# Three of four sequence transforms computed as cosine and sine halves in a spectral MLP kernel

## The chip, the cores and the metric

The kernel runs on one core of a Trainium2 chip. Five engines work side by side: TensorE (PE, matrix products; PEld is its weight load, which overlaps), VectorE (DVE), ScalarE (ACT), GpSimd (POOL) and SyncE (SP, which issues DMAs). The metric is the device time of one execution in microseconds (us), the median of several runs. Lower is better.

## The reference

```python
# x: (4, 3008, 256); w_in: (256, 2048); w_out: (2048, 256)
X = np.fft.fft(x, axis=1)
X = np.fft.fft(X, axis=2)
attn = X.real.astype(np.float32)          # two-dimensional transform, real part
h = attn.reshape(-1, 256) @ w_in
g = h * (1.0 / (1.0 + np.exp(-h)))
out = (g @ w_out).astype(np.float32)
```

## The kernel before

The transform over the 256 features is folded into `w_in` once, at the start; the transform over the 3008 rows is done on the chip as matrix products. Because the result is real and symmetric, only 1506 sequence frequencies of each of the four batches are made. They fall into four classes (`CLASS`, line 40): class 0 with 376 columns, class 1 with 378, classes 2 and 3 with 376 each. Sixteen transforms (batch b, class k, number c = 4b + k) feed a two-layer network that runs over columns in chunks: one chunk per class in batch 0, then three chunks of 502 columns for each other batch.

**Precision.** Products are made in fp32r with operands split into a high and a low part, so each logical product is three matmuls: high by high, high by low, low by high. `xh`, `xl` are the parts of a transform's operand; `uvh`, `uvl` those of its result, on which the network works.

**A step.** The main loop (from line 735) runs over the steps (chunk, f), f from 0 to 15, each for 128 hidden units. On PE a step issues `first` (six matmuls, lines 409 to 411) and `second` of the step three earlier (`LAG`; twelve matmuls, lines 463 to 470). DVE does three sums from PSUM in `act` (lines 420 to 422), ACT the SiLU and a rounding (433, 434), DVE the low part in `rest` (446).

**A turn.** At 15 fixed steps (`turns`, lines 683 to 691) a transform is issued on PE after `second` (`transform`, line 327), between two steps. The first of all transforms (batch 0, class 0) is made apart, at the start. The result goes to one of the two PSUM buffers `pq`, which `first` uses too, in turn. Then `spread` (line 367) empties it: ACT writes `uvh` (380), ACT copies row 0 to a small tile `row` (383), from which a DMA of SP's queue broadcasts it to 128 partitions as `ub` (384), and DVE writes `uvl` (387). The buffer is needed again by `first` two steps later. `ub` and the parts of `uv` are needed where their chunk begins, four steps after the turn at the least.

**A transform's matmuls.** Classes 0, 2 and 3 multiply three blocks of operand rows (`x3`, made by `operand`, line 250) by three table blocks of 376 columns, for two halves i of the features, each as three matmuls: 18 matmuls of 376 columns. Class 1 makes its even and odd outputs apart: 30 matmuls of 190 or 188 columns. Every matmul has its own weight load of 128 columns; the operand is the weight, and the table moves. `operand` runs in pieces between steps on DVE, ACT rounds to `xh` (315), and POOL makes `xl` (322).

**Order.** Everything is issued in an order written out by hand: each engine works its own queue strictly in that order, and side work is handed out by budgets per step (`drain`, line 490).

Of the kernel before, what the change touches and what calls it, by code (L numbers as in the profile page):

```python
# [24 lines left out]
F32 = mybir.dt.float32  # L25
F32R = mybir.dt.float32r
# [5 lines left out]
AF = mybir.ActivationFunctionType  # L32
ALU = mybir.AluOpType
# [3 lines left out]
Q4, H = S // 4, S // 8  # L37
NC = 1506
NT = B * NC
CLASS = ((0, 376), (376, 378), (754, 376), (1130, 376))  # L40
# [10 lines left out]
def fft_mlp(ctx, tc, x1, x2, x2_first, w_in, w_out, te, to, t2, t2f, rot1, rot2, dft, out):  # L51
    nc = tc.nc
    ctx.enter_context(tc.manual_schedule())
    tt = nc.vector.tensor_tensor
# [34 lines left out]
    t2f_sb = wts.tile([128, 2, 3, 376], F32, tag="t2", name="t2f")[:, 0]  # L89
    rot_sb = [wts.tile([128, 2, 2], F32, name=f"rot_sb{i}") for i in range(2)]  # L90

    wo_raw, wo_wide = {}, {}
# [58 lines left out]
    ends = slice(0, 129, 128)  # L151


    def fold_sums(k, i, ps=every):
        tt = nc.gpsimd.tensor_tensor
        sm = fold_tile("sm", k, i)[ps]
        gs = [raw_x.pop((k, i, h))[ps] for h in range(2)]

        def finish(h):
            nc.scalar.activation(sm[:, h, :, ends], gs[h][:, 0:2, ends], AF.Copy)  # L160

        for h, g in enumerate(gs):
            tt(g[:, 0:2], g[:, 0:2], g[:, 2:4], op=ALU.add)
            tt(sm[:, h, :, 1:128], g[:, 0:2, 1:128], g[:, 0:2, 129:], op=ALU.add)
            tt(sm[:, h, :, 129:], g[:, 0:2, 1:128], g[:, 0:2, 129:], op=ALU.subtract)
            yield 9
        finish(0)
        yield 9
        finish(1)
        ready.add(("sm", k, i, ps.stop))  # L170
# [79 lines left out]
    def operand(c):  # L250
# [8 lines left out]
        x3 = xf[:, :768].rearrange("p (a d) -> p a d", a=3)  # L259
        if k == 0:  # L260
            sm, sm2 = folded["sm", 0, b], folded["sm", 1, b // 2]
            tt(x3[:, 0:2, 0:129], sm[:, :, 0, 0:129], sm[:, :, 1, 0:129], op=ALU.subtract)
            for h in range(2):
                tt(x3[:, 1 - h, 129:], sm[:, h, 0, 129:], sm[:, h, 1, 129:], op=ALU.subtract)
            yield 0.7
            for h in range(2):
                rows = (lo, up)[h]
                tt(x3[rows, 2, 0:129], sm2[hs, h, 0, 0:129], sm2[hs, h, 1, 0:129], op=ALU.subtract)
                tt(x3[rows, 2, 129:], sm2[hs, 1 - h, 0, 129:], sm2[hs, 1 - h, 1, 129:], op=ALU.subtract)
            yield 0.8  # L270
        elif k == 1:
            sm, sm2 = folded["sm", 0, b], fold_tile("sm", 1, b // 2)
            piece = 0.3
            tt(sm[:, :, 0], sm[:, :, 0], sm[:, :, 1], op=ALU.add)
            yield piece
            if b:
# [18 lines left out]
            yield piece  # L295
            for par, op in ((0, ALU.add), (1, ALU.subtract)):
                tt(l0[:, par, 0:129], sm[:, 0, 0:129], sm[:, 1, 0:129], op=op)
                tt(l0[:, 1 - par, 257:], sm[:, 0, 129:], sm[:, 1, 129:], op=op)
                yield piece
                tt(c0[lo, par, 0:129], sm2[hs, 0, 0, 0:129], sm2[hs, 1, 0, 0:129], op=op)  # L300
                tt(c0[up, 1 - par, 129:], sm2[hs, 0, 0, 129:], sm2[hs, 1, 0, 129:], op=op)
                yield piece
        else:
            ri, ri2 = folded["ri", 0, b], folded["ri", 1, b // 2]
# [22 lines left out]
    def transform(c, po):  # L327

        b, k = divmod(c, 4)
        x = operands.pop(c)  # L330
        n = CLASS[k][1]
        def sl(a):
            return slice(a, a + 128)

        def product(dst, terms, part):

            w = dst.shape[-1]
            for j, (rows, a, t, blk) in enumerate(terms):
                for p in range(2 - part):
                    nc.tensor.matmul(dst, x[part][rows, sl(a)], t[rows, p, blk, :w], start=j + p + part == 0,  # L340
                                     stop=part == 1 and j == len(terms) - 1)

        if k == 1:
            for i in range(2):
                for par, t, at, m in ((0, tabs["te"], 0, 190), (1, tabs["to"], 190, 188)):
                    l, z = 384 * par, 768 + 256 * par
                    if i == 0:
                        terms = [(every, l, t, 0), (every, z, t, 2)]
                    else:
                        terms = [(every, l + 128, t, 0), (every, l + 256, t, 1), (every, z + 128, t, 2)]  # L350
                    for part in range(2):
                        product(po[:, i, at:at + m], terms, part)
        else:
            t = tabs[{0: "t2", 2: "te", 3: "to"}[k]]
            for part in range(2):
                for i in range(2):
                    product(po[:, i, :n], [(every, 256 * a + 128 * i, t, a) for a in range(3)], part)

    chunks = {}

# [6 lines left out]
    def spread(c, po):  # L367

        b, k = divmod(c, 4)
        o, n = CLASS[k]  # L370
        o += b * NC
        parts = []
        for j, (at, m) in enumerate(zip(STARTS, CHUNKS)):
            lo, hi = max(o, at), min(o + n, at + m)
            if lo < hi:
                uvh, uvl, ub, _, _ = chunk(j)
                src, dst = slice(lo - o, hi - o), slice(lo - at, hi - at)
                parts.append((uvh[:, :, dst], uvl[:, :, dst], ub[:, dst], src))
        for uvh, _, _, src in parts:
            nc.scalar.activation(uvh, po[:, :, src], AF.Copy)  # L380
        for _, _, ub, src in parts:
            row = fold_p.tile([1, 512], F32, tag="half", name="row", bufs=3)[:, :src.stop - src.start]
            nc.scalar.activation(row, po[0:1, 1, src], AF.Copy)  # L383
            nc.sync.dma_start(
                out=ub, in_=row.unsqueeze(0).to_broadcast([1, 128, src.stop - src.start]))
        for uvh, uvl, _, src in parts:
            tt(uvl, po[:, :, src], uvh.bitcast(F32), op=ALU.subtract)  # L387


    def spread_first(po):  # L390
        uvh, uvl, ub, n, _ = chunk(0)
# [331 lines left out]
    for q, n in enumerate((0, 1, 2, 3, 4, 5, 7, 9)):  # L723
# [6 lines left out]
        if q >= FULL // 2:  # L730
            fills.setdefault(n - 1, []).append((clear_wo, q))
            after.setdefault(n + 1, []).append((high_wo, q))
            fills.setdefault(n + 2, []).append((low_wo, q))

    for n in range(len(steps) + LAG):
        c, f = steps[min(n, len(steps) - 1)]
        if n < len(steps):
# [46 lines left out]
    return base % S, (-base) % S  # L784


_S1 = np.arange(128)
_S2 = np.concatenate([np.arange(128, 189), [188] * 3])


def _tables():
    w1 = np.where(_S1 == 0, 0.5, 1.0)[:, None]
    w2 = np.where(_S2 == 188, 0.5, 1.0)[:, None]
    w2[61:] = 0

    def cs(m):
        def f(s, fn):
            return fn(2 * np.pi * (np.outer(s, m) % 752) / 752)

        t = np.zeros((128, 3, len(m)))  # L800
        t[:, 0], t[:, 1] = w1 * f(_S1, np.cos), -w1 * f(_S1, np.sin)
        t[:64, 2], t[64:, 2] = w2 * f(_S2, np.cos), -w2 * f(_S2, np.sin)
        return t

    m = np.arange(376)

    def g(s):
        return np.cos(2 * np.pi * (np.outer(s, 2 * m + 1) % 1504) / 1504)

    t2 = np.zeros((128, 3, 376))  # L810
    t2[:, 0], t2[:, 1] = w1 * g(_S1), w1 * g(H - _S1)
    t2[:64, 2], t2[64:, 2] = w2 * g(_S2), w2 * g(H - _S2)

    def rot(s):
        b = 2 * np.pi * np.stack([s, H - s], 1) / S
# [12 lines left out]
    got = {  # L828
        "te": parts(cs(np.arange(0, 752, 2))), "to": parts(cs(np.arange(1, 752, 2))), "t2": parts(t2), "t2f": t2,
        "rot1": rot(_S1), "rot2": np.concatenate([rot(_S2)] * 2), "dft": dft,  # L830
    }
    return {k: np.ascontiguousarray(v, dtype=np.float32) for k, v in got.items()}
# [15 lines left out]

def _columns():

    m = np.arange(376)
    k = np.concatenate([4 * m + 2, 8 * np.arange(190), 8 * np.arange(188) + 4, 8 * m + 1, 8 * m + 5])
    neg = np.concatenate([m % 2 == 1, np.ones(378, bool), np.zeros(752, bool)])
    keep = np.arange(NC) != 376 + 189
    k1 = np.where(neg, -k, k) % S
    return keep, (-k1) % S, k1
# [28 lines left out]
```

## Time and profile before

| | us |
|---|---|
| median of 3 runs | 878.06 |
| lowest and highest | 877.62, 878.19 |
| profiled execution, whole time | 877.21 |
| its span, first to last instruction | 875.4 |
| PE busy in it | 866.1 (99%) |
| DVE busy | 706.2 (81%) |
| ACT busy | 508.9 (58%) |
| POOL busy | 197.9 (23%) |

A busy PE is not a PE at its peak, since matmuls are pipelined and their recorded durations overlap. What a matmul costs the engine is read from the spacing of the starts, or from the chain of waits, where each piece stands with the time that it adds.

### The profile page before, as it was taken

The numbers are of one execution on the slowest core, as the hardware profiler recorded it, in microseconds if no ns is written. First come the engines' busy times: TensorE is split into PE (matmuls) and PEld (weight loads), VectorE is DVE, ScalarE is ACT, GpSimd is POOL, SyncE is SP. The second block draws the span as 40 slices with busy tenths as digits, with TensorE's granted clock in tenths as the row PEclk, the third lists the DMA queues.
The fourth block names the chain that finished last, engine by engine and source line by source line (L and its number), as shares of the span: only waits on it lengthen the run. The fifth ranks groups of instructions, "written<-read, shape, count | busy, mean of one in ns | idle before, by whom it ended". The sixth has DMA issues, their size and how long they took to land.

```text
span 875.4 us, 11058 instructions
## 1 busy us (share of the span) xinstructions
PE 866.1 (99%) x4138; PEld 750.2 (86%) x4138; DVE 706.2 (81%) x994; ACT 508.9 (58%) x646; POOL 197.9 (23%) x243
## 2 busy tenths in 40 slices
PE   7999999999999999999999999999999999999998
PEld 6789999999998888888888888888888888888886
DVE  5999888888897887879778877888877877777774
ACT  4677756565765564557566455557546555455554
POOL 3475541312522220243312310050300110000000
PEclk9999999999999999999999999999999999999999
DMA  9955342236231433224225201323011021200101
GB/s 333 313 177 84 106 53 53 37 58 93 10 106 26 76 77 58 44 11 112 34 30 124 9 1 50 56 48 57 1 8 49 0 10 48 10 0 5 44 1 47
DMA packets 23413, 53.81 MB, mean 61 GB/s; under 512 B 3648, under 2 KB 12224, under 8 KB 22976
## 3 DMA queue, kind: packets, MB, share of 16 engines
q1 hardware_dynamic: 19632, 38.62, 20.4%
q0 software_dynamic: 3728, 14.49, 8.6%
q8 instruction: 32, 0.52, 0.3%
q14 instruction: 21, 0.17, 0.1%
HBM read 37.86 MB, written 12.34 MB: 57 GB/s over the span
## 4 chain that ended last, share of the span: by engine, by line
PE 97%; DMA 1%; DVE 1%; SPq 1%; issue 0%; ACT 0%; DVEq 0%
PE acc L470 20%; PE acc L464 20%; PE acc L463 20%; PE pq L409 10%; PE pq L410 10%; PE pq L411 10%; PE pq L340 5%; PE acc L461 2%; DMA minus<-in_x_dram 1%; PE pw L533 1%; PE pq L597 0%; SPq L74 0%; SPq L569 0%; DVE sm L204 0%; DVE sm L200 0%
## 5 line engine op out<-in xcount | busy, mean ns | idle before, releaser
L433 ACT ACTIVATE h<-h 128x1004 f32<-128x1004 f32 (+3 forms) x204 | 199.3, 977 | 303.6 <-DVE h L422 300.4
L463 PE MATMUL acc<-gh,woh 128*128 128x502 f32 (+2 forms) x808 | 302.2, 374 | 0.0
L464 PE MATMUL acc<-gh,wol 128*128 128x502 f32 (+2 forms) x808 | 302.2, 374 | 0.0
L446 DVE TENSOR_TENSOR gl<-h,gh 128x1004 fp32r<-128x1004 f32 (+3 forms) x204 | 237.9, 1167 | 14.7 <-ACT gh L434 14.0
L420 DVE SCALAR_TENSOR_TENSOR h<-ub,a,pq 128x502 f32<-128x502 f32 (+2 forms) x208 | 144.8, 696 | 96.7 <-PE pq L411 92.5
L470 PE MATMUL acc<-gl,woh 128*128 128x502 f32 (+2 forms) x808 | 210.3, 374 | 0.0
L434 ACT ACTIVATE gh<-h 128x1004 fp32r<-128x1004 f32 (+3 forms) x204 | 199.4, 977 | 6.5
L464 PEld LDWEIGHTS acc<-gh,wol 128*128 128x128 f32 x808 | 152.4, 189 | 22.4
L463 PEld LDWEIGHTS acc<-gh,woh 128*128 128x128 f32 x808 | 152.0, 188 | 22.3
L470 PEld LDWEIGHTS acc<-gl,woh 128*128 128x128 f32 x808 | 149.6, 188 | 23.2
L409 PE MATMUL pq<-uv,abh 128*128 128x502 f32 (+2 forms) x416 | 157.7, 379 | 0.0
L410 PE MATMUL pq<-uv,abh 128*128 128x502 f32 (+2 forms) x416 | 154.8, 372 | 0.0
L411 PE MATMUL pq<-uv,abl 128*128 128x502 f32 (+2 forms) x416 | 154.6, 372 | 0.0
L421 DVE TENSOR_TENSOR h<-h,pq 128x502 f32<-128x502 f32 (+2 forms) x208 | 132.7, 638 | 7.2
L422 DVE TENSOR_TENSOR h<-h,pq 128x502 f32<-128x502 f32 (+2 forms) x208 | 132.6, 638 | 7.2
L322 POOL TENSOR_TENSOR xl<-xf,xh 128x256 fp32r<-128x256 f32 x53 | 53.0, 1027 | 365.4 <-ACT xh L315 306.1
L409 PEld LDWEIGHTS pq<-uv,abh 128*128 128x128 f32 x416 | 78.1, 188 | 12.3 <-DVE h L422 0.5
L410 PEld LDWEIGHTS pq<-uv,abh 128*128 128x128 f32 x416 | 78.2, 188 | 11.7
L411 PEld LDWEIGHTS pq<-uv,abl 128*128 128x128 f32 x416 | 78.1, 188 | 11.4
L234 POOL TENSOR_TENSOR ri<-ri,raw 128x256 f32<-128x256 f32 x24 | 23.1, 978 | 57.6 <-ACT ri L229 57.3
L478 ACT ACTIVATE o<-acc 128x502 f32<-128x502 f32 (+2 forms) x52 | 27.9, 559 | 9.8 <-PE acc L470 7.7
L387 DVE TENSOR_TENSOR uv<-pq,uv 128x752 fp32r<-128x752 f32 (+4 forms) x21 | 14.5, 716 | 21.2 <-ACT row L383 21.1
(113 smaller groups left out, 472.5 us busy)
## 6 DMA issues: line engine op xcount, KB each, us to landing
raw<-in_x_dram SPq DMA_DIRECT2D x22, 512.0 KB, 6.3
raw<-in_x_dram POOLq DMA_DIRECT2D x20, 512.0 KB, 7.5
out_dram<-o SPq DMA_DIRECT2D x36, 251.0 KB, 2.2
win<-in_w_in_dram SPq DMA_DIRECT2D x8, 512.0 KB, 8.1
wo<-in_w_out_dram SPq DMA_DIRECT2D x8, 512.0 KB, 8.0
out_dram<-o SPq DMA_DIRECT2D x12, 188.0 KB, 2.3
ub<-row SPq DMA_DIRECT2D x8, 188.0 KB, 8.6
te<-in_te_dram POOLq DMA_DIRECT2D x1, 1128.0 KB, 5.5
```

The source lines that it names most:

```text
L409: nc.tensor.matmul(po, abh[:, i, fs], uvh[:, i, :n], start=True, stop=False)
L410: nc.tensor.matmul(po, abh[:, i, fs], uvl[:, i, :n], start=False, stop=False)
L411: nc.tensor.matmul(po, abl[:, i, fs], uvh[:, i, :n], start=False, stop=True)
L420: stt(p[:, :n], ub[:, :n], a128[f // 2][:, f % 2:f % 2 + 1], pq[:, 0, :n], op0=ALU.mult, op1=ALU.add)
L421: tt(h[:, 0, :n], p[:, :n], pq[:, 1, :n], op=ALU.add)
L422: tt(h[:, 1, :n], p[:, :n], pq[:, 1, :n], op=ALU.subtract)
L433: nc.scalar.activation(h[:, sg, :n], h[:, sg, :n], AF.Silu)
L434: nc.scalar.activation(gh[:, sg, :n], h[:, sg, :n], AF.Copy)
L446: tt(gl[:, sg, :n], g[:, sg, :n], gh[:, sg, :n].bitcast(F32), op=ALU.subtract)
L463: nc.tensor.matmul(po, wo[0][f // 2][:, f % 2, es], gh[:, sg, :n], start=f == 0, stop=False)
L464: nc.tensor.matmul(po, wo[1][f // 2][:, f % 2, es], gh[:, sg, :n], start=False, stop=False)
L470: nc.tensor.matmul(accs[c][i][:, :n], wo[0][f // 2][:, f % 2, es], gl[:, sg, :n], start=False, stop=f == NF - 1)
```

## The change

For classes 0, 2 and 3 the tables keep only half of the output columns (`w`, 188, or 190 for class 2). The transform writes two parts side by side into the same PSUM tile: for classes 2 and 3 a cosine part and a sine part, for class 0 the part of the even and of the odd rows. The first operand block is multiplied by the table of the first part, `w` columns wide, the second block by that of the second part, and the third block, which holds the remaining rows of both, by a table of `2 * w` columns. `spread` then copies the second part to SBUF (ACT, tile `q`), makes sum and difference on DVE into a new SBUF tile `wide`, and takes `uvh` and the broadcast row from `wide`; the low part `uvl` is made one step later, after the next `act`. Output columns come in another order, so the host tables and the gather of the output are permuted to match. Class 1 keeps its products; only its table layout differs.

```diff
-_S1 = np.arange(128)
+_S1 = np.concatenate([np.arange(0, 128, 2), np.arange(1, 128, 2)])
...
 # fold_sums
-            tt(sm[:, h, :, 129:], g[:, 0:2, 1:128], g[:, 0:2, 129:], op=ALU.subtract)
+            tt(sm[:, 1 - h, :, 129:], g[:, 0:2, 1:128], g[:, 0:2, 129:], op=ALU.subtract)
 # operand, class 0
-            tt(x3[:, 0:2, 0:129], sm[:, :, 0, 0:129], sm[:, :, 1, 0:129], op=ALU.subtract)
-            for h in range(2):
-                tt(x3[:, 1 - h, 129:], sm[:, h, 0, 129:], sm[:, h, 1, 129:], op=ALU.subtract)
-            yield 0.7
-            for h in range(2):
-                rows = (lo, up)[h]
-                tt(x3[rows, 2, 0:129], sm2[hs, h, 0, 0:129], sm2[hs, h, 1, 0:129], op=ALU.subtract)
-                tt(x3[rows, 2, 129:], sm2[hs, 1 - h, 0, 129:], sm2[hs, 1 - h, 1, 129:], op=ALU.subtract)
+            for par, src in enumerate((lo, up)):
+                for h, dst in enumerate((lo, up)):
+                    tt(x3[dst, par], sm[src, h, 0], sm[src, h, 1], op=ALU.subtract)
+                yield 0.8
+            for h, dst in enumerate((lo, up)):
+                tt(x3[dst, 2], sm2[hs, h, 0], sm2[hs, h, 1], op=ALU.subtract)
             yield 0.8
 # transform
-        def product(dst, terms, part):
+        def product(dst, a, t, at, part, start=False, stop=False):
             w = dst.shape[-1]
+            for p in range(2 - part):
+                nc.tensor.matmul(dst, x[part][:, a:a + 128], t[:, p, at:at + w], start=start and p + part == 0,
+                                 stop=stop and part == 1)
...
-            t = tabs[{0: "t2", 2: "te", 3: "to"}[k]]
+            t, w = {0: (tabs["t2"], 188), 2: (tabs["te"], 190), 3: (tabs["to"], 188)}[k]
             for part in range(2):
                 for i in range(2):
-                    product(po[:, i, :n], [(every, 256 * a + 128 * i, t, a) for a in range(3)], part)
+                    both = po[:, i, :2 * w], 512 + 128 * i, t, 2 * w, part
+                    if part == 0:
+                        product(*both, start=True)
+                    product(po[:, i, :w], 128 * i, t, 0, part)
+                    product(po[:, i, w:2 * w], 256 + 128 * i, t, w, part)
+                    if part:
+                        product(*both, stop=True)
 # spread
+        if k == 1:
+            wide = po
+        else:
+            wide = xs.tile([128, 2, 376], F32, tag="wide", name="wide")
+            w, m, skip = (190, 189, 1) if k == 2 else (188, 188, 0)
+            q = fold_p.tile([128, 2, 190], F32, tag="half", name="q", bufs=3)
+            nc.scalar.activation(q[:, :, :w], po[:, :, w:2 * w], AF.Copy)
+            tt(wide[:, :, :m], po[:, :, :m], q[:, :, :m], op=ALU.add)
+            tt(wide[:, :, m:], po[:, :, skip:skip + n - m], q[:, :, skip:skip + n - m], op=ALU.subtract)
         for uvh, _, _, src in parts:
-            nc.scalar.activation(uvh, po[:, :, src], AF.Copy)
+            nc.scalar.activation(uvh, wide[:, :, src], AF.Copy)
         for _, _, ub, src in parts:
-            row = fold_p.tile([1, 512], F32, tag="half", name="row", bufs=3)[:, :src.stop - src.start]
-            nc.scalar.activation(row, po[0:1, 1, src], AF.Copy)
+            row = wide[0:1, 1:2, src]
+            if k == 1:
+                row = fold_p.tile([1, 1, 512], F32, tag="half", name="row", bufs=3)[:, :, :src.stop - src.start]
+                nc.scalar.activation(row, po[0:1, 1:2, src], AF.Copy)
...
-        for uvh, uvl, _, src in parts:
-            tt(uvl, po[:, :, src], uvh.bitcast(F32), op=ALU.subtract)
+        def lower_parts():
+            for uvh, uvl, _, src in parts:
+                tt(uvl, wide[:, :, src], uvh.bitcast(F32), op=ALU.subtract)
+        if k == 1:
+            lower_parts()
+        return k != 1 and lower_parts
 # main loop
             act(c, f, fills.get(n, ()))
+            if lowers:
+                lowers = lowers()
...
-            spread(turn, new)
+            lowers = spread(turn, new)
 # tables: 3 blocks of 376 columns become 5 blocks of w (te, to) or 4 of 188 (t2)
-            tabs[name] = pool.tile([128, 2, 3, 376], F32R, name=name)
+            tabs[name] = pool.tile([128, 2, t.shape[-1]], F32R, name=name)
-        tabs["t2"] = wts.tile([128, 2, 3, 376], F32R, tag="t2", name="t2")
+        tabs["t2"] = wts.tile([128, 2, 752], F32R, tag="t2", name="t2")
```

## Rows read from the trace of the kernel before

**Rows 1.** Page: busy us of each engine, share of span, instructions.
```profile
PE 866.1 (99%) x4138; PEld 750.2 (86%) x4138; DVE 706.2 (81%) x994; ACT 508.9 (58%) x646; POOL 197.9 (23%) x243
```

**Rows 2.** Waits of PE, all of them: us in total, times, longest.
```profile
PE pq L597 <- DVE xf L207: 2.0, 2, 1.1
PE pq L587 <- POOL wof L573: 1.8, 1, 1.8
PE pw L533 <- DVE wf L82: 1.5, 1, 1.5
```

**Rows 3.** Page: chain that ended last, shares of the span by line.
```profile
PE acc L470 20%; PE acc L464 20%; PE acc L463 20%; PE pq L409 10%; PE pq L410 10%; PE pq L411 10%; PE pq L340 5%; PE acc L461 2%; DMA minus<-in_x_dram 1%; PE pw L533 1%; PE pq L597 0%; SPq L74 0%; SPq L569 0%; DVE sm L204 0%; DVE sm L200 0%
```

**Rows 4.** The same chain in order of time: start us, us, what.
```profile
121.83 0.69 PE acc L470 x4
122.53 3.08 PE pq L340 x18
...
435.81 3.33 PE pq L340 x30
...
487.39 0.92 PE acc L470 x4
...
749.70 3.09 PE pq L340 x18
```

**Rows 5.** Line 340, weight loads: ns min/median/max, first and last start, forms.
```profile
L340 PEld LDWEIGHTS pq<-te,xh x88: 187/188/192, 65.6 to 699.0; 128*128 128x128 f32 x88
```

**Rows 6.** Span and mean granted TensorE clock of the core.
```profile
core 0: 875.4 us, clock 1.000
```

**Rows 7.** Timeline after a class 2 turn: start us, us, instruction [idle before].
```profile
489.96 1.21 DVE L446 TENSOR_TENSOR gl<-h,gh 128x1004 fp32r<-128x1004 f32 x1 [0.76 <-ACT gh L434]
...
491.24 0.40 PE L409 MATMUL pq<-uv,abh 128*128 128x502 f32 x1
...
491.44 0.86 ACT L380 ACTIVATE uv<-pq 128x500 fp32r<-128x500 f32 x2 [1.51 <-PE pq L340]
...
492.73 1.00 DVE L387 TENSOR_TENSOR uv<-pq,uv 128x500 fp32r<-128x500 f32 x2 [1.56 <-ACT row L383]
...
494.32 0.73 DVE L420 SCALAR_TENSOR_TENSOR h<-ub,a,pq 128x502 f32<-128x502 f32 x1
...
495.34 0.39 PE L409 MATMUL pq<-uv,abh 128*128 128x502 f32 x1
```

**Rows 8.** Timelines of four engines after the class 2 turn of batch 0.
```profile
125.45 0.33 PE L409 MATMUL pq<-uv,abh 128*128 128x378 f32 x1
128.57 0.34 PE L409 MATMUL pq<-uv,abh 128*128 128x378 f32 x1
...
125.65 0.80 ACT L380 ACTIVATE uv<-pq 128x752 fp32r<-128x752 f32 x1 [1.64 <-PE pq L340]
...
126.83 0.48 SPq L384 DMA_DIRECT2D ub<-row  x1
...
136.06 0.61 DVE L420 SCALAR_TENSOR_TENSOR h<-ub,a,pq 128x376 f32<-128x376 f32 x1 [0.49 <-PE pq L411]
```

**Rows 9.** DMA issues: count, KB each, median us from issue to landing.
```profile
ub<-row SPq DMA_DIRECT2D x8, 188.0 KB, 8.6
```

**Rows 10.** By tile: ns min/median/max of instructions like the added ones.
```profile
L394 ACT ACTIVATE uv<-pq x2: 451/468/484, 25.1 to 25.9; 128x376 fp32r<-128x376 f32 x2
L396 DVE TENSOR_TENSOR uv<-pq,uv x2: 540/545/550, 25.6 to 26.7; 128x376 fp32r<-128x376 f32 x2
...
L309 DVE TENSOR_TENSOR xf<-ri x8: 408/415/422, 110.7 to 705.7; 64x256 f32<-64x256 f32 x8
```

**Rows 11.** Timelines of POOL and PE before the class 0 turn of batch 1.
```profile
193.97 2.85 POOL L322 TENSOR_TENSOR xl<-xf,xh 128x256 fp32r<-128x256 f32 x3 [29.60 <-ACT xh L315]
...
202.07 1.19 PE L340 MATMUL pq<-t,xl 128*128 128x376 f32 x6
```

**Rows 12.** Waits of DVE, the longest: us in total, times, longest.
```profile
DVE h L420 <- PE pq L411: 92.5, 130, 1.3
```

More of the change, by code (lines that the diff above doesn't have):

```diff
@@ L88, in fft_mlp @@
     tabs = {}
-    t2f_sb = wts.tile([128, 2, 3, 376], F32, tag="t2", name="t2f")[:, 0]
+    t2f_sb = wts.tile([128, 1504], F32, tag="t2", name="t2f")[:, :1128].rearrange("p (a k) -> p a k", a=3)
     rot_sb = [wts.tile([128, 2, 2], F32, name=f"rot_sb{i}") for i in range(2)]
@@ L272, in operand @@
             sm, sm2 = folded["sm", 0, b], fold_tile("sm", 1, b // 2)
-            piece = 0.3
+            piece, h0 = 0.3, 1 if b else 0
             tt(sm[:, :, 0], sm[:, :, 0], sm[:, :, 1], op=ALU.add)
@@ L297, in operand @@
                 tt(l0[:, par, 0:129], sm[:, 0, 0:129], sm[:, 1, 0:129], op=op)
-                tt(l0[:, 1 - par, 257:], sm[:, 0, 129:], sm[:, 1, 129:], op=op)
+                tt(l0[:, 1 - par, 257:], sm[:, h0, 129:], sm[:, 1 - h0, 129:], op=op)
                 yield piece
                 tt(c0[lo, par, 0:129], sm2[hs, 0, 0, 0:129], sm2[hs, 1, 0, 0:129], op=op)
-                tt(c0[up, 1 - par, 129:], sm2[hs, 0, 0, 129:], sm2[hs, 1, 0, 129:], op=op)
+                tt(c0[up, 1 - par, 129:], sm2[hs, h0, 0, 129:], sm2[hs, 1 - h0, 0, 129:], op=op)
                 yield piece
@@ L330, in transform @@
         x = operands.pop(c)
-        n = CLASS[k][1]
-        def sl(a):
-            return slice(a, a + 128)
-        def product(dst, terms, part):
+        def product(dst, a, t, at, part, start=False, stop=False):
             w = dst.shape[-1]
[L338 to L341, printed above, removed]
+            for p in range(2 - part):
+                nc.tensor.matmul(dst, x[part][:, a:a + 128], t[:, p, at:at + w], start=start and p + part == 0,
+                                 stop=stop and part == 1)
@@ L343, in transform @@
         if k == 1:
             for i in range(2):
[L345 to L350, printed above, removed]
+                for par, t, dst in ((0, tabs["te"], po[:, i, :190]), (1, tabs["to"], po[:, i, 190:378])):
+                    w = dst.shape[-1]
+                    l, z = 384 * par + 128 * i, 768 + 256 * par + 128 * i
@@ L351, in transform @@
                     for part in range(2):
-                        product(po[:, i, at:at + m], terms, part)
+                        product(dst, l, t, 0, part, start=True)
+                        if i:
+                            product(dst, l + 128, t, w, part)
+                        product(dst, z, t, 4 * w, part, stop=True)
         else:
-            t = tabs[{0: "t2", 2: "te", 3: "to"}[k]]
+            t, w = {0: (tabs["t2"], 188), 2: (tabs["te"], 190), 3: (tabs["to"], 188)}[k]
             for part in range(2):
@@ L378, in spread @@
                 parts.append((uvh[:, :, dst], uvl[:, :, dst], ub[:, dst], src))
+        if k == 1:
[7 more added lines that the diff above has]
+            tt(wide[:, :, m:], po[:, :, skip:skip + n - m], q[:, :, skip:skip + n - m], op=ALU.subtract)
         for uvh, _, _, src in parts:
-            nc.scalar.activation(uvh, po[:, :, src], AF.Copy)
+            nc.scalar.activation(uvh, wide[:, :, src], AF.Copy)
         for _, _, ub, src in parts:
-            row = fold_p.tile([1, 512], F32, tag="half", name="row", bufs=3)[:, :src.stop - src.start]
-            nc.scalar.activation(row, po[0:1, 1, src], AF.Copy)
-            nc.sync.dma_start(
-                out=ub, in_=row.unsqueeze(0).to_broadcast([1, 128, src.stop - src.start]))
-        for uvh, uvl, _, src in parts:
-            tt(uvl, po[:, :, src], uvh.bitcast(F32), op=ALU.subtract)
+            row = wide[0:1, 1:2, src]
+            if k == 1:
+                row = fold_p.tile([1, 1, 512], F32, tag="half", name="row", bufs=3)[:, :, :src.stop - src.start]
+                nc.scalar.activation(row, po[0:1, 1:2, src], AF.Copy)
+            nc.sync.dma_start(out=ub, in_=row.to_broadcast([1, 128, src.stop - src.start]))
+        def lower_parts():
[4 more added lines that the diff above has]
+        return k != 1 and lower_parts
     def spread_first(po):
@@ L733, in fft_mlp @@
             fills.setdefault(n + 2, []).append((low_wo, q))
+    lowers = None
     for n in range(len(steps) + LAG):
@@ L784, in _rows @@
     return base % S, (-base) % S
-_S1 = np.arange(128)
-_S2 = np.concatenate([np.arange(128, 189), [188] * 3])
+_S1 = np.concatenate([np.arange(0, 128, 2), np.arange(1, 128, 2)])
+_S2 = np.concatenate([np.arange(128, 189, 2), [188], np.arange(129, 188, 2), [188] * 2])
+_PAD = [31, 62, 63]
+_M0 = np.concatenate([np.arange(188), 375 - np.arange(188)])
+_M2 = np.concatenate([np.arange(189), 376 - np.arange(1, 188)])
 def _tables():
@@ L793, in _tables @@
     w2 = np.where(_S2 == 188, 0.5, 1.0)[:, None]
-    w2[61:] = 0
+    w2[_PAD] = 0
     def cs(m):
@@ L798, in f @@
             return fn(2 * np.pi * (np.outer(s, m) % 752) / 752)
-        t = np.zeros((128, 3, len(m)))
-        t[:, 0], t[:, 1] = w1 * f(_S1, np.cos), -w1 * f(_S1, np.sin)
-        t[:64, 2], t[64:, 2] = w2 * f(_S2, np.cos), -w2 * f(_S2, np.sin)
+        w = len(m)
+        t = np.zeros((128, 5 * w))
+        t[:, :w], t[:, w:2 * w] = w1 * f(_S1, np.cos), -w1 * f(_S1, np.sin)
+        t[:64, 2 * w:3 * w], t[64:, 3 * w:4 * w] = w2 * f(_S2, np.cos), -w2 * f(_S2, np.sin)
+        t[:, 4 * w:] = t[:, 2 * w:3 * w] + t[:, 3 * w:4 * w]
         return t
-    m = np.arange(376)
     def g(s):
[L808 to L812, printed above, removed]
+        return np.cos(2 * np.pi * (np.outer(s, 2 * _M0 + 1) % 1504) / 1504)
+    t2f = np.zeros((128, 3, 376))
+    t2f[:, 0], t2f[:, 1] = w1 * g(_S1), w1 * g(H - _S1)
+    t2f[:64, 2], t2f[64:, 2] = w2 * g(_S2), w2 * g(H - _S2)
+    t2 = np.zeros((128, 752))
+    for k in range(2):
+        own, tail = slice(64 * k, 64 * k + 64), slice(32 * k, 32 * k + 32)
+        for h in range(2):
+            dst = slice(64 * h, 64 * h + 64)
+            t2[dst, 188 * k:188 * k + 188] = t2f[own, h, :188]
+            t2[64 * h + 32 * k:64 * h + 32 * k + 32, 376 + 188 * k:564 + 188 * k] = t2f[dst, 2, :188][tail]
     def rot(s):
@@ L828, in _tables @@
     got = {
-        "te": parts(cs(np.arange(0, 752, 2))), "to": parts(cs(np.arange(1, 752, 2))), "t2": parts(t2), "t2f": t2,
+        "te": parts(cs(2 * np.arange(190))), "to": parts(cs(2 * np.arange(188) + 1)), "t2": parts(t2), "t2f": t2f,
         "rot1": rot(_S1), "rot2": np.concatenate([rot(_S2)] * 2), "dft": dft,
@@ L849, in _columns @@
 def _columns():
-    m = np.arange(376)
-    k = np.concatenate([4 * m + 2, 8 * np.arange(190), 8 * np.arange(188) + 4, 8 * m + 1, 8 * m + 5])
-    neg = np.concatenate([m % 2 == 1, np.ones(378, bool), np.zeros(752, bool)])
+    k = np.concatenate([4 * _M0 + 2, 8 * np.arange(190), 8 * np.arange(188) + 4, 8 * _M2 + 1, 8 * _M0 + 5])
+    neg = np.concatenate([_M0 % 2 == 1, np.ones(378, bool), np.zeros(752, bool)])
     keep = np.arange(NC) != 376 + 189
```

## The prediction

> **What bounds the kernel now.** Read the engines' busy shares first: PE is busy for 99% of the span, DVE, the next compute engine, for 81% [rows 1]. A busy PE can still be one that waits in small pieces, so the waits of PE come second: there are three in all, 5.3 us together, on lines of the opening part, and none in the loop over steps [rows 2]. Third, the chain that ended last: line after line of PE work, with the transforms (line 340) at 5% of the span [rows 3]. DVE, for its part, waits for PE in 130 of its 208 steps [rows 12]. So in the loop PE runs without a gap, everything else follows it, and the end moves by what PE's instruction stream gets shorter, as long as no new wait opens.
>
> **What a matmul costs PE.** The recorded durations overlap, so I take the chain in order of time, where a piece stands with what it adds [rows 4]. Four matmuls of 502 columns add 0.92 us, 0.229 each; four of 376 add 0.69, 0.173 each; the 18 of a transform of class 0, 2 or 3 add 3.09, 0.172 each (eleven such pieces, the first and the last of them in the group); the 30 narrow ones of a class 1 transform, of 190 and 188 columns, add 3.33, **0.111 each**. From 502 to 376 columns the price falls by 0.057 us for 126 columns, 0.45 ns a column. On that line 188 columns would cost 0.172 - 188 x 0.45 ns = 0.087. They cost 0.111, so something other than columns holds narrow matmuls back by 0.024. The granted clock is 1.000 throughout, the 2.4 GHz level [rows 6], so it is not the clock. Each matmul has a weight load of its own; it is recorded at 0.188 us [rows 5] but loads overlap the stream.
>
> The Trainium skill, "TensorE: Matmul & The Clock Gate", section "LDWEIGHTS (loading the stationary operand)", puts a load at the columns of the weight divided by 1.2 GHz, an estimate of 107 ns for 128 columns: a rule that speaks against halving the moving columns below that. By it the sum below would be 8.6 us rather than 8.0; the narrow row agrees with it within 4 ns.
>
> **The transform, the only term that sets the end.** The count of matmuls stays at 18. In the high part each of the two halves i issues two of 2w columns and four of w; in the low part one and two. That is 6 wide (376, or 380 in class 2) and 12 narrow (188 or 190). Price: 6 x 0.172 + 12 x 0.111 = 1.03 + 1.33 = 2.36 us, against 3.09. It saves 0.73 us in each of 11 transforms: **8.0 us**. The narrow price is taken from class 1, since that is the same instruction, width, weight size and destination; the bounds are 0.087 (the column line), giving 12 x 0.085 = 1.02 us a transform and 11.2 in all, and 0.188 (loads one behind the other as recorded), giving 12 x -0.016 = -0.19 and 2.1 us lost. The first transform of all, class 1's four and the 208 steps are not touched.
>
> **Emptying the PSUM buffer.** This is the part with new work, and it lies behind PE. Before, in a 502-column turn, the next step's first matmul starts at 491.24, ACT begins `uvh` at 491.44, and the last read of the buffer, DVE's `uvl`, ends at 493.73; the buffer is wanted at 495.34, 4.10 us after 491.24 [rows 7]. In 376-column steps it is wanted after 3.12 us [rows 8]. After the change: 0.20 to ACT's start, 0.47 for `q` (376 elements from PSUM, as line 394), then two DVE operations of 376 elements from PSUM, 0.55 each as line 396 [rows 10]: 1.77 us. That is earlier than before by about 0.7, because `uvl` no longer reads PSUM. Is DVE free? Its rest operation before it ends at 489.96 + 1.21 = 491.17 [rows 7]; the transform will end 0.73 earlier, about 490.5, so ACT's `q` runs to about 491.2 and DVE starts `wide` without a wait. ACT then waits about a microsecond for `wide` before `uvh`; queued behind it is only the next step's SiLU, which waits for DVE sums that end later. Cost on the path: nothing, with 1.3 us of cover in a 376-column step and 2.3 in a 502-column one.
>
> **DVE and ACT in total.** DVE gains two operations of 0.55 us at most and keeps a `uvl` of the same size: 1.1 x 11 = 12 us. It has 169 us idle, and in a turn PE still adds 2.36 us in which no step's sums fall due. The `uvl` now comes after the next `act`; in that step `rest` has nothing left to do, since the turn did it ahead, so it falls into the hole. Before, line 420 of the step after a turn came at 494.32, 1.6 us or so behind PE [rows 7]; with the row copies' wait gone, I expect less. ACT gains 11 copies and loses 14 row copies: even.
>
> **The broadcast row.** The DMA waits for both DVE operations: 0.47 + 2 x 0.55 = 1.57 us after ACT's start, against 126.83 - 125.65 = 1.18 before [rows 8], so 0.4 later. SP's queue behind it holds loads and output stores, delayed by as much. It lands after 8.6 us [rows 9], before at about 135.4, where line 420 of the next chunk starts at 136.06; the 0.6 of cover shrinks to 0.2 in the tightest turn. Were it lost, DVE would start late by some tenths; its three sums take about 1.8 us and their buffer is wanted two steps on, so PE would not see it. Cost nothing.
>
> **The class 0 operand.** Six DVE operations on 64 partitions, 0.42 us each as line 309 [rows 10], in three pieces rather than two, so `xh` and `xl` come one step (3.1 us) later, three times in all. For batch 1 the three `xl` pieces on POOL end at 196.8, and the low matmuls start at 202.07 [rows 11]: 5.3 us of cover becomes about 2, less 0.2 or so because the high part shortens. Later batches begin eight steps ahead instead of five. Cost nothing; if that cover were gone, the loss is at most a microsecond or two in one turn. The swapped half in `fold_sums` has the same size, the tables shrink, and the late `uvl` is wanted three or more steps on: nothing.
>
> **Sum.** 877.21 - 8.0 = 869.2 for an execution like the profiled one. The median stands 0.85 above that execution: 878.06 - 8.0 = **870.0**.
>
> **Rivals.**
> (a) *Narrow matmuls go by columns.* If the 0.111 comes from how class 1 is arranged (thirty narrow ones in a row) and narrow ones beside wide ones find their weights already loaded, the price is 0.087 and the time 878.06 - 11.2 = 866.9. For it: a wide matmul leaves the loader time to spare. Against it: here too narrow ones come in runs of four and two. A price between is possible. Chance 0.10.
> The Trainium skill, "TensorE: Matmul & The Clock Gate", section "Back-to-back issue gap", gives columns over 2.4 GHz plus 2.5 ns for a matmul alone, an estimate of 81 ns for 188 and 159 for 376, and so 10.3 us saved; the trace's 172 and 111 are both above it.
> (b) *The buffer's release takes over.* ACT, then DVE, then DVE is a longer chain of engines than before. PE stalls when it takes over 3.12 us (three turns) or 4.10 (eight); the gain of 0.73 is gone from 3.85 and 4.83 on. At 4.1 and 5.1 each turn costs 0.98, less 0.73: 11 x 0.25 = 2.8 us slower, 880.8. For it: DVE may be held up where POOL works. Against it: 1.77 us by the rows, and each part would have to be nearly three times as long. Chance 0.03 for that end, 0.06 for a part of the gain lost (872 to 876).
> (c) *Loads bind at their recorded length*, 0.188: 878.06 + 2.1 = 880.2. It decides as soon as a narrow matmul costs more than 0.172. Against it stand the 120 narrow matmuls of class 1 at 0.111. Chance 0.01.
> (d) *Nothing on PE shortens in effect*, because another engine has become the bound: 878. DVE's 130 waits for PE speak against it. Chance 0.02.
>
> **How the numbers follow.** Forecast 0.78, rivals as above. The range reaches from (a), with some rounding, to a loss of a quarter of a microsecond in each turn: 866.5 to 873.0. A change of about 0.2% (1.8 us) is what a measurement can tell here. Faster by more than that: the forecast, (a) and most of the partial loss, 0.93; slower: the end of (b) and (c), 0.04; the same: 0.03.
>
> **What would show it.** Right: PE busy near 858 with 4138 matmuls as before; line by line in the chain, eleven transforms of 2.36 us where 3.09 stood; still no wait of PE in the loop; DVE waiting for PE as often. Wrong: PE waiting for a DVE line of `spread` two steps after a turn (b); transforms of 2.1 us (a) or of 3.3 (c); PE waiting for `xl` at a class 0 turn.

## The result, and the profile after

| | before | after | ratio, 95% interval |
|---|---|---|---|
| first measurement, median us | 877.84 | 870.41 | 0.9915 [0.9898, 0.9932] |
| measured again, median us | 877.53 | 870.82 | 0.9923 [0.9910, 0.9935] |
| profiled execution, us | 877.21 | 869.4 | |
| its span, us | 875.4 | 867.6 | |

By the medians, the change makes the kernel 6.7 to 7.4 us faster. The forecast was 870.0 with a gain of 8.0.

The page of the profile after, first the busy time of each engine (beside [rows 1]), then the shares of the chain that ended last, by engine:

```profile
PE 858.7 (99%) x4138; PEld 742.4 (86%) x4138; DVE 716.9 (83%) x1013; ACT 510.7 (59%) x643; POOL 201.4 (23%) x243
...
PE 93%; DVE 4%; DMA 1%; SPq 0%; issue 0%; ACT 0%; DVEq 0%
```

PE has as many matmuls as before and is busy for 7.4 us less. But 4% of the chain now lies on DVE, where it was 1% before:

```profile
PE 97%; DMA 1%; DVE 1%; SPq 1%; issue 0%; ACT 0%; DVEq 0%
```

The waits say where; beside [rows 2], all waits of PE after (us in total, times, longest):

```profile
PE pq L616 <- DVE xf L208: 2.0, 2, 1.1
PE pq L606 <- POOL wof L592: 1.8, 1, 1.8
PE pq L428 <- DVE h L441: 1.2, 2, 0.9
```

The third line is new: `first` (line 428) waits for the last of DVE's three sums (line 441), 1.2 us in two pieces. The chain in order of time after (start us, us, what), beside [rows 4]:

```profile
64.75 3.33 PE pq L335 x30
...
121.35 2.38 PE pq L335 x18
...
173.49 2.37 PE pq L335 x18
...
226.52 3.33 PE pq L335 x30
...
742.63 2.37 PE pq L335 x18
```

A transform of class 0, 2 or 3 adds 2.37 where it added 3.09. Ten of the eleven stand in this chain; at the class 0 turn of batch 1 the chain runs over DVE instead, and the timeline of PE has the eleventh:

```profile
197.47 1.71 PE L335 MATMUL pq<-t,xh 128*128 128x376 f32 x12
...
199.84 0.34 PE L428 MATMUL pq<-uv,abh 128*128 128x376 f32 x1
```

From its start to that of the next step pass 199.84 - 197.47 = 2.37 us too. So eleven transforms take 7.9 us less. Class 1 adds 3.33 as before. The opening part, up to the first line of the chain above, happened to be 1.2 us shorter in this execution (64.75 against 65.94 before); the experiments show that this is not the change's. What does not depend on it is read from a later point: from the class 2 turn of batch 0 to the end of the span it was 875.4 - 122.53 = 752.9 us before and is 867.6 - 121.35 = 746.3 after, 6.6 less. That is 7.9 of the transforms less some 1.3 of the new wait.

The timeline after a class 2 turn, beside [rows 7]:

```profile
486.37 0.38 PE L428 MATMUL pq<-uv,abh 128*128 128x502 f32 x1
486.56 0.49 ACT L389 ACTIVATE q<-pq 128x380 f32<-128x380 f32 x1 [0.78 <-PE pq L335]
...
487.09 0.55 DVE L390 TENSOR_TENSOR wide<-pq,q 128x378 f32<-128x378 f32 x1
...
487.56 0.54 DVE L391 TENSOR_TENSOR wide<-pq,q 128x374 f32<-128x374 f32 x1
...
488.12 1.12 SPq L399 DMA_DIRECT2D ub<-wide  x2
...
488.68 0.73 DVE L439 SCALAR_TENSOR_TENSOR h<-ub,a,pq 128x502 f32<-128x502 f32 x1
...
490.46 0.39 PE L428 MATMUL pq<-uv,abh 128*128 128x502 f32 x1
```

The buffer is read for the last time at 487.56 + 0.54 = 488.10, 1.73 us after the next step began on PE, and wanted at 490.46. The new emptying is hidden here, with the cover that was worked out.

### The profile page after: what moved, and what is told of

It is laid out like the page before. It is cut to its first block, busy times and chain, and to the rows that moved or that the text cites. A ratio compares the mean times of both kernels' runs of the same rounds, so it can differ in the third digit from the quotient of the medians.

```text
span 867.6 us, 11079 instructions
## 1 busy us (share of the span) xinstructions
PE 858.7 (99%) x4138; PEld 742.4 (86%) x4138; DVE 716.9 (83%) x1013; ACT 510.7 (59%) x643; POOL 201.4 (23%) x243
## 4 chain that ended last, share of the span: by engine, by line
PE 93%; DVE 4%; DMA 1%; SPq 0%; issue 0%; ACT 0%; DVEq 0%
PE acc L489 19%; PE acc L483 19%; PE acc L482 19%; PE pq L428 10%; PE pq L429 10%; PE pq L430 10%; PE pq L335 4%; PE acc L480 2%; DMA minus<-in_x_dram 1%; DVE gl L465 1%; DVE h L439 1%; PE pw L552 1%; DVE h L440 1%; DVE h L441 1%; PE pq L616 0%
## 5 line engine op out<-in xcount | busy, mean ns | idle before, releaser
L144 POOL DMA_DIRECT2D raw<-in_x_dram x22 | 18.9, 898 | 108.4 <-DMA raw<-in_x_dram 102.8
```

## Experiments

### What holds a narrow matmul at 0.111 us

The price was taken from class 1 without knowing its cause. Two runs changed the width of the narrow matmuls, `v` columns in place of `w`:

```diff
-                    product(po[:, i, :w], 128 * i, t, 0, part)
-                    product(po[:, i, w:2 * w], 256 + 128 * i, t, w, part)
+                    product(po[:, i, :v], 128 * i, t, 0, part)
+                    product(po[:, i, 2 * w - v:2 * w], 256 + 128 * i, t, w, part)
```

> The changed kernel with its twelve narrow matmuls of each turn at other widths: 128 columns in class 0, 64 in class 2, 256 in class 3 (so parts are incomplete, or overlap). Theory T1, the weight load sets a floor of 0.111 us under a narrow matmul: class 0 and class 2 transforms stay at 2.37 us, class 3 goes by the column line, 12 x 0.118 + 1.03 = 2.45. Theory T2, columns plus an addition of 0.024 for narrow ones: class 0 12 x 0.084 + 1.03 = 2.04, class 2 12 x 0.055 + 1.03 = 1.69, class 3 12 x 0.142 + 1.03 = 2.73.

> As widths_a with 32 columns in class 0, 160 in class 2 and 220 in class 3. T1: all three at 2.37 us (220 columns would be 0.102 by the column line, under the floor). T2: class 0 12 x 0.041 + 1.03 = 1.52, class 2 12 x 0.098 + 1.03 = 2.21, class 3 12 x 0.126 + 1.03 = 2.54.

The chain of the first (64 columns in class 2, then 256 in class 3, then 128 in class 0):

```profile
278.86 2.37 PE pq L335 x18
...
330.36 2.45 PE pq L335 x18
...
381.94 2.37 PE pq L335 x18
```

and of the second (160, 220 and 32 columns):

```profile
278.69 2.37 PE pq L335 x18
...
330.19 2.36 PE pq L335 x18
...
381.69 2.37 PE pq L335 x18
```

From 32 to 220 columns a narrow matmul costs the same; at 256 the transform takes 2.45 us, as the column line says. So there is a floor of 0.111 us, and T2, columns plus an addition, falls. What the floor is, the next run asked: the same widths as the changed kernel, fewer weight columns (`m`).

```diff
-                nc.tensor.matmul(dst, x[part][:, a:a + 128], ...
+                nc.tensor.matmul(dst, x[part][:, a:a + m], ...
```

> The changed kernel with its narrow matmuls at the same width (188 or 190) but with fewer weight columns: 64 in class 0, 32 in class 2, 96 in class 3 (the other features of a part are left out). T1 with a load that goes by weight columns: the floor sinks to 0.056, 0.028 and 0.083, so all three classes go by the column line, 12 x 0.087 + 1.03 = 2.07 us a transform, and the time falls by 11 x 0.30 = 3.3 us. T1 with a load that doesn't depend on columns, and T2: 2.37 us as before.

Its chain (32 weight columns, then 96, then 64):

```profile
278.27 2.15 PE pq L335 x18
...
329.56 2.16 PE pq L335 x18
...
380.85 2.14 PE pq L335 x18
```

The floor does hang on the weight load, but the transform fell to 2.15, not to 2.07, and by the same amount for 32, 64 and 96 columns. The 0.08 us that stayed led to a sharper form: a load runs while the matmul before it streams, so a matmul pays for the load of the one that comes next. Three of the twelve narrow ones stand before a wide one, whose load still has 128 columns.

> Sharpens the load theory after the run with fewer weight columns, which gave 2.15 in all three classes where 2.07 was expected. T3: a matmul costs the larger of its own columns (the line of 0.45 ns a column) and the load of the matmul that comes next; a load goes by weight columns, 0.111 for 128. Then in that run only 3 of the 12 narrow matmuls, those before a wide one, still paid 0.111: 9 x 0.087 + 3 x 0.111 + 1.03 = 2.15. Here class 0 has narrow ones of 64 columns with 64 weight columns: 9 x 0.056 + 0.333 + 1.03 = 1.87; class 2 64 columns with 32 weight columns: 9 x 0.031 + 0.333 + 1.03 = 1.64; class 3 188 columns with 64 weight columns, the wide ones moved to both ends so that only one narrow matmul stands before a wide one: 11 x 0.087 + 0.111 + 1.03 = 2.10. Rival T4, a narrow matmul with fewer than 128 weight columns simply costs 0.093: class 0 and 2 at 2.15 or by columns, class 3 at 2.15. Parts of the outputs are left out.

Its chain (class 2, class 3, class 0):

```profile
277.82 1.65 PE pq L335 x18
...
328.61 2.11 PE pq L335 x18
...
379.85 1.89 PE pq L335 x18
```

1.64, 2.10 and 1.87 were worked out, 1.65, 2.11 and 1.89 measured; T4, which has class 3 at 2.15, is out. A matmul here costs the larger of its own columns, 0.45 ns each, and the load of the next matmul's weights, 0.111 us for 128 columns. By this rule the order of wide and narrow ones cannot help while all weights have 128 columns, since each narrow one hides only part of the load behind it. Rival (a) of the prediction, narrow ones finding their weights already loaded, is answered by this.

### Where the new wait comes from

The changed kernel was run again, beside kernels that each take one thing away.

> The changed kernel as it is, timed again beside the next three. The profile of the changed kernel has eleven transforms of 2.37 us instead of 3.09 (7.9 us less), an opening part that happened to be 1.2 us shorter (first transform at 64.75 instead of 65.94), and a new wait of PE of 1.2 us after the class 0 turn of batch 1. If the opening varies from run to run by itself, the time here is 869 to 871.5 and the profile's first transform may start anywhere from 64.5 to 66.5; if the change shortened the opening, it starts near 64.7 again.

The first class 1 turn now started at 65.93, so the short opening was chance; over all runs of this study it starts between 64.75 and 66.10. The wait of 1.2 us came back, 0.9 and 0.3. Since the opening varies by as much as the wait is worth, the runs below are compared by the stretch **from the class 2 turn of batch 0 to the class 1 turn of batch 1**, from the chain: 105.96 us before (122.53 to 228.49), 105.17 after, 105.18 in the run again. Three transforms are in it, so without a new wait it would be 105.96 - 3 x 0.72 = 103.8. The four runs with other widths and weights, whose transforms have other lengths, have the wait too, and the more of it the shorter their transforms: 1.3 in both runs with other widths, 1.6 and 1.8 us in the two with fewer weight columns. All runs that follow, with the starts from their chains and their waits of PE for line 441:

| kernel | class 2 turn, us | class 1 turn, us | stretch | wait |
|---|---|---|---|---|
| before | 122.53 | 228.49 | 105.96 | none |
| after | 121.35 | 226.52 | 105.17 | 1.2 |
| after, again | 122.47 | 227.65 | 105.18 | 1.2 |
| class 1 operand two steps later | 122.66 | 226.76 | 104.10 | 0.3 |
| old emptying | 122.48 | 226.77 | 104.29 | 0.3 |
| wide products, new emptying | 123.39 | 230.23 | 106.84 | 0.7 |
| old class 0 operand | 122.87 | 226.89 | 104.02 | 0.3 |
| class 1 operand one step later | 121.92 | 227.79 | 105.87 | 1.7 |
| low part on POOL | 121.78 | 226.37 | 104.59 | 0.6 |
| POOL's fold later | 123.55 | 227.32 | 103.77 | none |

> The changed kernel with the operand of the class 1 transform of batch 1 begun two steps later, at step 5 of its chunk instead of step 3. Theory S1: the new wait of PE (1.2 us near 209) comes from DVE work piled up after that turn, of which this operand's pieces (2.1 us between two steps) are the last straw; then no wait of PE stands in the loop and the time is 1.2 us lower, about 869.2. Rivals S2 (the sum and difference of the new emptying alone) and S3 (the heavier class 0 operand alone): the wait stays at about 1 us, and the time is that of the changed kernel.

```diff
-    turns, begins = {}, {..., 5: (3, 3), 6: (3, 15)}
+    turns, begins = {}, {..., 5: (3, 5), 6: (3, 15)}
```

Measured 869.89 us, ratio to before 0.9914 [0.9901, 0.9928]. The wait fell to 0.3 us; but the class 1 transform itself took 3.59 instead of 3.33 us, since its low operand now came late. The interval overlaps that of the changed kernel.

> The new narrow products, but the PSUM buffer emptied as before: no copy q, no sum and difference, row copied by ACT, low part at once. It leaves out the sum and difference, so its columns are parts and not outputs. Forecast of the prediction (the emptying is hidden): the time is that of the changed kernel less at most the 1.2 us of its new wait, 869 to 870.5. Theory S2: the wait of PE near 209 is gone. Rival (b), the emptying costs on the path: several us faster than the changed kernel.

```diff
-        if k == 1:
-            wide = po
-        else:
+        wide = po
+        if False:
...
-        if k == 1:
-            lower_parts()
-        return k != 1 and lower_parts
+        lower_parts()
+        return False
```

(The row copy of class 1 is used for all classes.) Measured 869.51, ratio 0.9911 [0.9898, 0.9925], 1.3 us less than the changed kernel beside it: the sum, the difference and the copy cost about its wait in all eleven turns together, and the wait went with them, down to 0.3. The intervals of the two overlap; the stretch, 0.9 us shorter, shows the difference more clearly.

> The new emptying with products of 376 columns for all 18 matmuls, so the transform takes as long as before. It computes wrong sums in place of the parts. Forecast: eleven transforms of 3.09 us, no wait of PE in the loop of more than a few tenths, 877.5 to 878.5, the time of the kernel before. Rival (b): 879 or more, with waits of PE for DVE two steps after turns.

```diff
-                    product(po[:, i, :w], 128 * i, t, 0, part)
-                    product(po[:, i, w:2 * w], 256 + 128 * i, t, w, part)
+                    product(po[:, i, :376], 128 * i, t, 0, part)
+                    product(po[:, i, :376], 256 + 128 * i, t, w, part)
```

Measured 878.50, ratio 1.0012 [1.0003, 1.0021]: the other half of the change by itself makes the kernel 1 us slower. It lies at the upper end of what was forecast; 0.9 of it is in the stretch, with 0.7 us of waits of PE in two pieces, each of a few tenths as was expected. A wait of 0.9 on line 403 lies outside the stretch and is told of below. Rival (b) as a large loss falls.

> The changed kernel with the class 0 operand made as before (two pieces, seven operations, 2.1 us on DVE instead of three pieces and 2.6); its operand rows then lie in the wrong order. Theory S3: PE's wait of 1.2 us after the class 0 turn of batch 1 is gone. S1 and S2: it stays at 0.5 us or more.

The edit puts the seven lines of `operand` before the change back in place of the six new ones. One execution took 869.79 us, with a wait of 0.3. So each of three different takings-away (S1, S2, S3) brought back 0.9 to 1.2 us of the stretch: none of them can be *the* cause, and each passed its own test. Two tries followed. One began the class 1 operand one step later instead of two:

> The class 1 operand of batch 1 begun one step later instead of two. With two steps the wait of PE fell from 1.2 to 0.3 us, but that class 1 transform took 3.59 instead of 3.33, since its low operand came late. S1: with one step the wait falls as well and the transform stays at 3.33; 869 to 870.5. If the pile of DVE work only moves, the wait is 0.6 to 1.2 us and the time that of the changed kernel, 870 to 871.

The edit is `5: (3, 4)`. Measured 871.65, ratio 0.9936 [0.9922, 0.9949]: the wait **grew** to 1.7 us, though DVE had the same work to do. The other took work off DVE:

> The low part of a turn's result made on POOL instead of DVE, which the new tile in SBUF allows. It takes 0.94 us off DVE in each of eleven turns. If the 1.2 us wait of PE is DVE's total load in that stretch: the wait is 0.3 us or less and the time 869 to 870. Rival: POOL at work slows DVE beside it (the low part of the SiLU took 2.10 instead of 0.94 beside POOL in one run), and waits come back elsewhere: 870 to 872.

```diff
-                tt(uvl, wide[:, :, src], uvh.bitcast(F32), op=ALU.subtract)
+                (tt if k == 1 else nc.gpsimd.tensor_tensor)(uvl, wide[:, :, src], uvh.bitcast(F32), op=ALU.subtract)
```

Measured 870.75, ratio 0.9922 [0.9908, 0.9936]: 0.94 us less on DVE in every turn halved the wait to 0.6 and gained nothing that can be measured. That does not clear the amount of DVE work, since POOL got more to do in the same place. The timelines of DVE and POOL of the changed kernel, just before its wait, show another candidate:

```profile
204.99 1.37 DVE L403 TENSOR_TENSOR uv<-wide,uv 128x752 fp32r<-128x752 f32 x1
206.28 0.82 DVE L296 TENSOR_TENSOR xf<-sm 128x129 f32<-128x129 f32 x1
207.02 0.54 DVE L297 TENSOR_TENSOR xf<-sm 128x127 f32<-128x127 f32 x1
207.58 0.46 DVE L299 TENSOR_TENSOR xf<-sm 64x129 f32<-64x129 f32 x1
208.05 0.29 DVE L300 TENSOR_TENSOR xf<-sm 64x127 f32<-64x127 f32 x1
...
204.27 1.29 POOL L219 TENSOR_TENSOR raw<-raw 128x512 f32<-128x512 f32 x1 [3.84 <-DMA raw<-in_x_dram]
205.63 1.31 POOL L221 TENSOR_TENSOR raw<-raw 128x254 f32<-128x254 f32 x1
206.91 0.51 POOL L222 TENSOR_TENSOR raw<-raw 128x127 f32<-128x127 f32 x1
207.38 0.50 POOL L223 TENSOR_TENSOR raw<-raw 128x127 f32<-128x127 f32 x1
```

While POOL works on SBUF here, DVE's operations that take both inputs from SBUF stretch: the low part takes 1.37 us, the four operand pieces 2.1 in all. Each of the first four starts while an operation of POOL is under way and ends a while after that one has ended (POOL's first at 205.56, the low part 0.80 later; the second at 206.94, the first operand piece 0.16 later), as if it had stood until then. As soon as POOL is done, at 207.88, the fourth piece takes 0.29. In the kernel before, the low part ran beside POOL too, but read PSUM:

```profile
204.48 0.94 DVE L387 TENSOR_TENSOR uv<-pq,uv 128x752 fp32r<-128x752 f32 x1 [1.67 <-ACT row L383]
205.34 0.98 DVE L274 TENSOR_TENSOR sm<-sm 128x512 f32<-128x512 f32 x1
206.33 1.13 DVE L277 TENSOR_TENSOR sm<-sm 64x512 f32<-64x512 f32 x1
...
204.48 1.29 POOL L218 TENSOR_TENSOR raw<-raw 128x512 f32<-128x512 f32 x1 [5.03 <-DMA raw<-in_x_dram]
```

and took 0.94. The two operations behind it did read SBUF twice, and they took 0.98 and 1.13 beside POOL; away from POOL, in the changed kernel, the same two take 0.68 and 0.69. So DVE lost 0.74 us to POOL here before the change as well, without a wait of PE. After it the low part loses 0.43 and the four operand pieces 0.96, by their lengths in the next run, and DVE no longer has the time to spare. The last run leaves the order of PE and DVE as it is and moves POOL's fold alone (the ACT operations that belong to that fold come after 220 us with or without the edit):

```diff
-    fold("ri", 0, 1, 2, 14)
+    at(2, 14, load_x, 0, 1)
+    at(2, 18, add_x, 0, 1)
+    at(3, 8, add, pool_queue, ("ri", 0, 1), fold_diffs(0, 1))
```

> The changed kernel, with DVE's and PE's order untouched; only POOL's next fold (of batch 1, lines 219 to 223) is begun three steps later, so that it no longer runs beside DVE after the class 0 turn of batch 1. Theory S4: PE's wait of 1.2 us comes from DVE operations on SBUF that stretch beside POOL there (the low part of the result 1.37 us instead of 0.94, the four operand pieces behind it 2.1 in all instead of 1.2), not from the amount of DVE work. Then these have 0.94 and 1.2 again, the wait is 0.3 or less, from the class 2 turn of batch 0 to the class 1 turn of batch 1 pass 104.0 to 104.3 us instead of 105.2, and the time is about 869.5. If the amount of DVE work is the cause, the wait and the 105.2 stay.

Its DVE, at the same place:

```profile
207.16 0.93 DVE L403 TENSOR_TENSOR uv<-wide,uv 128x752 fp32r<-128x752 f32 x1
208.01 0.29 DVE L296 TENSOR_TENSOR xf<-sm 128x129 f32<-128x129 f32 x1
208.21 0.28 DVE L297 TENSOR_TENSOR xf<-sm 128x127 f32<-128x127 f32 x1
208.51 0.29 DVE L299 TENSOR_TENSOR xf<-sm 64x129 f32<-64x129 f32 x1
208.81 0.29 DVE L300 TENSOR_TENSOR xf<-sm 64x127 f32<-64x127 f32 x1
```

its chain:

```profile
123.55 2.38 PE pq L335 x18
...
227.32 3.33 PE pq L335 x30
```

and the last of its waits of PE:

```profile
PE pq L428 <- DVE uv L403: 1.0, 1, 1.0
```

The stretch is 227.32 - 123.55 = 103.8 us, the value without any wait, and the wait for line 441 is gone with all DVE work still there. S4 holds. It fits the two tries as well: with the class 1 operand one step later, that operand's first two operations fell beside POOL's fold and took 1.79 and 1.13 us instead of 0.68 and 0.69; with the low part on POOL (1.97 us there), the four operand pieces took 2.85 instead of 2.11. The amount of DVE work still counts, since less of it, or later, cured most of the wait too: by these runs the wait needs both, a DVE without slack and the stretch beside POOL. Measured 870.02, ratio 0.9909 [0.9892, 0.9925]. The trace shows the wait gone, but the intervals overlap: that it beats the changed kernel in time is not shown.

The wait that stands in its row is another, on line 403 after the class 1 turn of batch 0, where nothing of the change touches the work. It stood in eight of the twelve runs made after the result (0.9 to 1.0 us), and neither in the other four nor in the first profiles of the two kernels. Where it stands, as in the run with the old operand, the low part of the SiLU took 2.10 us beside POOL's line 119 at 1.30; where it does not, as in the changed kernel run again, 0.94 beside the same line at 2.08:

```profile
69.72 2.10 DVE L467 TENSOR_TENSOR gl<-h,gh 128x752 fp32r<-128x752 f32 x1 [0.69 <-ACT gh L455]
...
69.73 1.30 POOL L119 TENSOR_TENSOR wol<-wf,woh 128x512 fp32r<-128x512 f32 x1
```

```profile
70.32 0.94 DVE L465 TENSOR_TENSOR gl<-h,gh 128x752 fp32r<-128x752 f32 x1 [0.68 <-PE pq L430]
...
70.33 2.08 POOL L119 TENSOR_TENSOR wol<-wf,woh 128x512 fp32r<-128x512 f32 x1
```

Both start within 0.01 us of one another; one of them runs at its own length, the other waits for it. Which one it is differs between these runs, whose kernels are the same at this place, and with it a wait of PE of about 1 us comes or stays away.

The Trainium skill, "SBUF — State Buffer", section "Who interferes with whom", states this rule: a DVE instruction with two SBUF inputs and a GpSimd instruction that reads SBUF exclude one another, the first to issue goes through, and a DVE instruction with at most one SBUF input, outside the two-port modes, is not concerned. The rows above agree on who is concerned (0.94 us beside POOL with one input from PSUM, 1.37 and 2.10 with both from SBUF) and that one stands until the other is done; which of two that start together goes first, the recorded starts don't tell.

## Why the prediction was right or wrong

**The term that sets the end: right.** 6 x 0.172 + 12 x 0.111 = 2.36 us was worked out, 2.37 measured, in all eleven; 7.9 us of PE work fell away. Taking the price from the row of the same instruction, and not from the line through the wide ones, is what made the size right: by columns it would have been 11.2. The reason left open ("something other than columns") is the load of the next matmul's weights, 0.111 for 128 columns. The rule of the Trainium skill cited there, an estimate of 107 ns, is borne out by the runs with fewer weight columns: 64 of them cost 0.059 us, beside an estimate of 53 ns by that rule.

**Emptying the buffer: right.** 1.77 us from the next step's start, 1.73 measured; the broadcast row's DMA 1.57 after ACT's start, 488.12 - 486.56 = 1.56 measured. DVE's three sums come sooner behind PE after a turn, as expected: 488.68 where the step began at 486.37, against 494.32 for 491.24 [rows 7]. The run with the old emptying was 1.3 us faster, with overlapping intervals, and its stretch 0.9 us shorter: what this part costs is about the new wait, which is the next point.

**"Falls into the hole": wrong, by 1.2 us.** This is the step that failed, with the sentence "cost nothing" on the class 0 operand. The sign "still no wait of PE in the loop" failed with it. Summed over the span it held: DVE's busy time rose by 10.7 us where 12 were put down, and DVE waits for PE 125 times where it was 130 [rows 12]. These are the row of those waits and the piece of the chain where it passes to DVE:

```profile
DVE h L439 <- PE pq L430: 90.6, 125, 1.1
...
180.06 0.62 DVE h L439
```

But the low part was counted as unchanged by its size alone. It took 0.94 when it read PSUM. Now it reads `wide` in SBUF, beside POOL, and takes 1.37; the operand pieces behind it, which took both inputs from SBUF before too, meet POOL there with a DVE that had no slack left: from 180 us on the chain of the changed kernel runs over DVE, with one SiLU and its rounding on ACT in between, through the three longer pieces of the class 0 operand, to the waits that end at 210 and 214. The cover of `xl` at that turn, the other thing looked at, did hold: the three pieces on POOL end at 197.77 and the low matmuls start at 199.02, 1.25 us later where a little under 2 was expected. What the prediction named as a doubt under rival (b), "DVE may be held up where POOL works", was looked for in the buffer's chain, which reads PSUM and was not held up.

**The sum.** 8.0 us was forecast; 7.9 came from PE and 1.3 went to the new wait, which leaves 6.6. The second measurement's 6.7 is close to it and the first one's 7.4 above; the opening and the wait after the first turn vary by about a microsecond each. That the profiled execution came within 0.2 us of its forecast (869.4 beside 869.2) is luck: its opening was 1.2 us shorter by chance, and that made up for the new wait.

**Rivals.** (a) and (c) fall by the width and weight runs. (b) as a large loss falls; a part of the gain was lost, but less than the 872 to 876 put down for it, and not by the buffer's release. (d) falls: the time moved with PE's work.

## What to carry to other kernels

In a stream like this one, price a matmul by the larger of its own columns and the load of the weights that follow, and look for a row of the width you are going to: halving the columns from 376 to 188 took 35% off the price here, not half. When a result moves from PSUM to SBUF before the next DVE operation, that operation can become open to POOL, as the low part did here, so its duration must be taken from a row beside a busy POOL. Where three different removals each cure a wait, look for what they all shift in time; here moving POOL's fold alone, with the order of PE and DVE untouched, took the whole wait away.

## What the runs showed of the hardware

The floor under a narrow matmul is flat: 0.111 us from 32 to 220 columns with 128 weight columns, though each load is recorded at 0.188 [rows 5]. With 64 weight columns (class 0 of the last run on loads) it is (1.89 - 1.03 - 3 x 0.111) / 9 = 0.059. A DVE operation with both inputs in SBUF and POOL reading SBUF do not share: when they started within 0.01 us of one another, either DVE's 0.94 became 2.10 or POOL's 1.30 became 2.08, and the recorded starts, DVE's first by 0.01 both times, don't tell which.
